# Startup transposes in shared PSUM banks, a new base time for the planner, and two output tiles kept in PSUM: one change to a planned two-branch attention kernel

## The chip, the cores and the metric

The kernel runs on one core of a Trainium2 chip. The core has five engines that run side by side, each with its own instruction queue, worked off in order: TensorE (matrix products and transposes, written to PSUM), VectorE (DVE), ScalarE (ACT), GpSimd (POOL) and SyncE (SP, which here only issues DMAs). They wait for each other by semaphores. PSUM has eight banks of 128 partitions by 512 fp32 values; a matrix product can land only there, and only VectorE and ScalarE take results out of it here. The metric is the time of one execution in microseconds, as the device measures it; lower is better.

## The reference

Two attention branches run on the same input `x` of 2048 tokens by 512 values (bf16), 32 heads of 16, and are mixed by a gate per token:

```python
x = A_x
g = _sigmoid((x * gate_w).sum(-1, keepdims=True))
a = _A_ref(x, A_wqkv, A_wo)
b = _B_ref(x, B_wqkv, B_wo)
return g * a + (1 - g) * b
```

Branch A is full attention, without a mask:

```python
qkv = (x @ wqkv).reshape(B, S, 3, H, Dh).transpose(2, 0, 3, 1, 4)
scores = jnp.einsum("bhqd,bhkd->bhqk", q, k) * (Dh ** -0.5)
p = _softmax(scores, axis=-1)
o = jnp.einsum("bhqk,bhkd->bhqd", p, v)
return o.transpose(0, 2, 1, 3).reshape(B, S, D) @ wo
```

Branch B is local: each token sees itself and seven earlier tokens in steps of two (`W, dil = 8, 2`), with its own weights.

## The kernel before, in words

**Branch A.** Heads are taken four at a time (a group; `NG = 8`), queries 512 at a time (a chunk; `NC = 4`), which gives 32 periods. In a period the scores of a head against 128 keys (a unit) are one matmul of 32 rows, and 64 units make the period. Units are put together in sets of three and two (`set_sizes=(3, 2)`). A wide set lands in PSUM ring `rA` (three banks), a narrow one in `rB` (two banks); ScalarE takes the exponential of a whole set in one instruction into `pT`; then TensorE multiplies four units at a time with the values and adds into an accumulator of one bank. There are 684 sets. In most periods some units do not go through ScalarE: VectorE makes an approximate exponential of them by integer arithmetic (`p1`, and three shifted copies `sh`), and TensorE adds all four versions up.

The softmax is not shifted by its own maximum. The kernel instead appends to each key a bound on the keys' size: `k_bound` reduces the largest key values (`mx`), moves them between partitions with two tiny matmuls with a permutation (`sw`), takes the negative maximum (`ng`), and fills it into the key rows (`fill`). No score matmul of a head group can start before its fill.

**Branch B.** Tiles of 128 tokens. TensorE projects, VectorE copies keys and values to `kvs`, SyncE stores them to DRAM (`kv_scr`) and gathers them back shifted (`ksh`, `vsh`), GpSimd multiplies and adds, ScalarE does a small exponential per tile, some sums run as accumulating DMAs. TensorE transposes the result into `obt`.

**The start.** SyncE issues the loads: first chunk of `x`, A's key weights, the other three chunks, A's query and value weights, the gate vector and B's weights. TensorE transposes each chunk into `xT` in two halves (L612 to L637): the first half goes to ring `rA` and is copied out by ScalarE, the second half to ring `rB` and is copied out by VectorE. Then come the four key projections of head group 0, the first query projection (`q_proj(0, ...)`), the first value blocks (`v_proj(0, 4, ...)`), the bound and its fill, and the first score set.

**The end.** The last four output tiles cannot be finished before the last head groups are. For each of them the part that is already known is summed in PSUM in the last two periods and copied by VectorE into unused room of the key buffer as fp32 (`fa`). After the last exponential VectorE transposes the accumulator (`po1`), takes reciprocals, scales by the gate and transposes back (`po3`); TensorE does one more matmul per tile (`tail`), VectorE adds the kept part (`t_ev`), and SyncE stores the tile.

**What sets the order.** The order on each engine is not the order of the source. Every step is an `op` with an engine, an assumed duration, a due time, an earliest time (`rel`), dependences and the buffers that it takes (`tok`). `list_schedule` plays this through with its own clock: whenever an engine could start something, it picks the startable step with the earliest due time. For loads the assumed time until the data lies in place is `lat`. Due times of branch A follow from a base time `T0` and a pace of 0.465 per unit (`S0` are the starts of the periods); those of branch B follow from `b_start` and do not depend on `T0`. `misc` and `acc` name three shared PSUM banks; accumulators, projections and the scores for VectorE take them in turn. Where TensorE would be thin, the planner puts in matmuls with zeros (`zeros`). The order that comes out is then fixed by a chain of dependences on each engine. So a changed due time or duration at one place can move steps everywhere.

Of the kernel before, what the change touches and what calls it, by code (L numbers as in the profile page):

```python
# [9 lines left out]
ALU = mybir.AluOpType  # L10
AX = mybir.AxisListType
# [17 lines left out]
NG = 8  # L29
# [272 lines left out]
def kernel(  # L302
# [49 lines left out]
    def chain(bi):  # L352
        return chain_on("pe", bi)
# [21 lines left out]
    def mm_ct(out, lhsT, rhs, start, stop):  # L375
        mm(out, lhsT, rhs, start, stop)
# [32 lines left out]
    T0 = 17.0  # L409
# [76 lines left out]
    kmax = const.tile([128, NG], FP32, name="kmax")  # L486
# [89 lines left out]
    o_x[0] = op("sp", 0.5, load_x(0), -9.0, alloc=[xtok[0]], lat=5.5)  # L576
    o_wk = op("sp", 0.5, load_w(1), -8.9, lat=6.5)
    o_x[1] = op("sp", 0.5, load_x(1), -8.8, alloc=[xtok[1]], lat=7.5)
    o_x[2] = op("sp", 0.5, load_x(2), -8.7, alloc=[xtok[2]], lat=9.5)
    o_x[3] = op("sp", 0.5, load_x(3), -8.6, alloc=[xtok[3]], lat=11.0)  # L580
    o_wq = op("sp", 0.5, load_w(0), -8.5, lat=12.5)
    o_wv = op("sp", 0.5, load_w(2), -8.4, lat=13.0)
    o_bw = op("sp", 1.0, load_bw, -8.3, lat=19.0)
# [28 lines left out]
    o_xt = []  # L612
    for sc in range(NC):
        st = {}
        tk2 = [tok("rA", 1), tok("rB", 1)]

        def tr(half, sc=sc, st=st):
            def s():
                st[half] = ps.tile([128, 2, QW], BF16, tag=("rA", "rB")[half], bufs=1, name="pxt")
                for c in range(2):  # L620
                    for tt in range(TPC):
                        chain(nc.tensor.transpose(out=st[half][:, c, tt * 128:(tt + 1) * 128],  # L622
                                                  in_=xld[sc][:, tt, (2 * half + c) * 128:(2 * half + c + 1) * 128],
                                                  identity=ident[:]))
            return s

        def ev(half, sc=sc, st=st):
            def s():
                dst = xT[:, 2 * half:2 * half + 2, sc * QW:(sc + 1) * QW]
                src = st[half][:]  # L630
                if half == 0:
                    A.copy(out=dst, in_=src)
                else:
                    V.tensor_copy(out=dst, in_=src)
            return s
        t1 = op("pe", 0.6, tr(0), -5.0 + sc, deps=[o_x[sc], o_id], alloc=[tk2[0]], use=[xtok[sc]])
        t2 = op("pe", 0.6, tr(1), -4.9 + sc, deps=[t1], alloc=[tk2[1]], use=[xtok[sc]])  # L637
        o_xt.append([op("act", 1.0, ev(0), -5.0 + sc, deps=[t1], use=[tk2[0]]),
                     op("dve", 0.61, ev(1), -4.9 + sc, deps=[t2], use=[tk2[1]])])
# [24 lines left out]
    def k_bound(i, dl):  # L664
# [3 lines left out]
        def mx():  # L668
            V.tensor_reduce(out=kmax[:, i:i + 1], in_=kmax_all[:, i, :], axis=AX.X, op=ALU.max)
            V.tensor_copy(out=kmax_b[:, i:i + 1], in_=kmax[:, i:i + 1])  # L670
# [15 lines left out]
        a = op("dve", 0.4, mx, dl - 2.5, deps=o_kc[i])  # L686
# [61 lines left out]
    v_proj(0, 4, 0, 8, "misc", 6.0)  # L748
    v_proj(0, 4, 8, 8, "misc", 7.0)
# [9 lines left out]
    def q_proj(pi, tag, dl, rel=0.0):  # L759
# [15 lines left out]
        def ev():  # L775
            V.tensor_copy(out=qt_tiles[pi][:], in_=st["p1"][:])
# [7 lines left out]
        c = op("dve", 0.61, ev, dl - 0.5, deps=[b], use=[tk, tq])  # L784
        o_q[pi] = op("dve", 0.0, ab, dl, deps=[c], use=[tq], parts=SB(QW))

    q_proj(0, "acc", 2.5)
# [46 lines left out]
    for pi in range(2, NP, 2):  # L834
        q_pair(pi, S0[pi] - QD, S0[pi - 2] - 2.0)
# [558 lines left out]
    for t in range(NT):  # L1394
# [6 lines left out]
        dl = E + (4.0 + 4.0 * tt if last else 2.0 + 4.0 * tt)  # L1401

        def ab_part(k0, st=st, c_=c_, tt=tt, nh=nh):
            def s():
                if k0 == 0:
                    st["pf"] = misc_ps([128, D])
                for k in range(k0, min(k0 + 2, DC + nh)):
                    if k < DC:
                        mm_ct(st["pf"], obt_tiles[c_][:, k, tt * 128:(tt + 1) * 128], bwo[:, k, :], k == 0, k == DC + nh - 1)
                    else:  # L1410
                        mm_ct(st["pf"], oat_tiles[c_][:, k - DC, tt * 128:(tt + 1) * 128], woarr[:, k - DC, :], False,
                              k == DC + nh - 1)
            return s
# [13 lines left out]
        for k0 in range(0, DC + nh, 2):  # L1427
            nk = min(2, DC + nh - k0)
            a = op("pe", WAVE(nk), ab_part(k0), dl - 2.0 + 0.3 * k0, full=nk,
                   deps=[a] if k0 else [o_oat[NG * c_ + ng - 1], o_wo] + o_obt[t:t + 1],  # L1430
                   alloc=[tk] if k0 == 0 else [], use=([tk] if k0 else []) + [oat_tok[c_], obt_tok[c_]])
        if not last:
            tos = tok("osb", 2)
            a = op("dve", 0.61, ab_ev, dl, deps=[a], alloc=[tos], use=[tk])
            op("sp", 0.6, dout, dl + 1, deps=[a], use=[tos], lat=2.2)
        else:
            a = op("dve", 0.61, ab_ev, dl, deps=[a], use=[tk])
            tag = ("misc", "acc", "rB", "rA")[tt]
            otag = ("osb", "osb", "kvs", "kvs")[tt]
            tk, tos = tok(tag, 2 if tag == "misc" else 1), tok(otag, 2)  # L1440
            E2 = S0[NP]
# [9 lines left out]
            b = op("dve", 0.61, t_ev, E2 + 1 + tt, deps=[b, a], alloc=[tos], use=[tk])  # L1451
            op("sp", 0.6, dout, E2 + 2 + tt, deps=[b], use=[tos], lat=2.2)

# [45 lines left out]
```

## Time and profile before

| | us |
|---|---|
| median of three runs | 819.31 |
| the three runs | 816.12, 819.31, 819.32 |
| the profiled execution, its own time | 815.66 |
| its span | 813.9 |
| first exponential of branch A starts | 19.58 |
| last exponential of branch A starts, ends | 804.48, 805.13 |
| ScalarE busy | 785.7 (97%) |
| TensorE busy | 751.9 (92%) |
| VectorE busy | 690.2 (85%) |
| GpSimd busy | 633.8 (78%) |

Times in the profile count from the start of the span. A group line gives the source line of the helper that recorded the instruction, engine, operation, result and operands, shapes and how often; then busy time and mean duration, and after the second bar the idle time of the engine just before and what ended it. All VectorE, ScalarE and GpSimd operations go through one helper (L364) and all matmuls through another (L373), so the names of the tiles tell them apart: `ring` are score sets, `pT` exponentials, `misc_ps` whatever lies in the shared banks, `pxt` transposed chunks of `x`, `xld` and `pd_a` the loaded chunks (the fourth lies in `pd_a`), `wk` the copy of key weights, `z` zeros. In timelines the first two numbers of a line are start and duration of a run of equal instructions, the bracket at its end idle time before the run.

### The profile page before, as it was taken

The numbers are of one execution on the slowest core, as the hardware profiler recorded it, in microseconds if no ns is written. First come the engines' busy times: TensorE is split into PE (matmuls) and PEld (weight loads), VectorE is DVE, ScalarE is ACT, GpSimd is POOL, SyncE is SP. The second block draws the span as 40 slices with busy tenths as digits, with TensorE's granted clock in tenths as the row PEclk, the third lists the DMA queues.
The fourth block names the chain that finished last, engine by engine and source line by source line (L and its number), as shares of the span: only waits on it lengthen the run. The fifth ranks groups of instructions, "written<-read, shape, count | busy, mean of one in ns | idle before, by whom it ended". The sixth has DMA issues, their size and how long they took to land.

```text
span 813.9 us, 18012 instructions
## 1 busy us (share of the span) xinstructions
PE 751.9 (92%) x6962; PEld 246.2 (30%) x7018; DVE 690.2 (85%) x1080; ACT 785.7 (97%) x706; POOL 633.8 (78%) x1058
## 2 busy tenths in 40 slices
PE   8999999999999998999889999989989999898996
PEld 4333334324222222222222222323222222222322
DVE  5646776897887999989989899997988899898887
ACT  2999999999999999999999999999999999999995
POOL 3098969799899999999997794989769419899910
PEclk9999999999999999999999999999999999999998
DMA  7503071533544344443524407162440521522000
GB/s 261 143 2 118 2 172 50 135 86 100 132 118 112 95 114 131 103 127 93 149 55 119 126 17 171 45 162 54 91 125 12 124 92 49 147 59 72 1 2 27
DMA packets 58886, 77.22 MB, mean 95 GB/s; under 512 B 3744, under 2 KB 50848, under 8 KB 58800
## 3 DMA queue, kind: packets, MB, share of 16 engines
q1 hardware_dynamic: 52752, 54.05, 21.5%
q0 software_dynamic: 6048, 22.02, 14.6%
q8 instruction: 55, 0.90, 0.5%
q14 instruction: 31, 0.25, 0.1%
HBM read 43.78 MB, written 10.26 MB: 66 GB/s over the span
## 4 chain that ended last, share of the span: by engine, by line
ACT 46%; PE 28%; issue 18%; POOL 4%; DVE 3%; DMA 1%; SPq 0%; DVEq 0%; ACTq 0%
ACT pT L364 46%; PE misc_ps L373 19%; PE ring L373 8%; POOL prod L364 2%; POOL av L364 1%; DMA xld<-in_A_x_dram 1%; DVE kt_all L364 1%; ACT lg L364 1%; DVE pd_a L364 1%; PE pxt L622 0%; DVE wkv L364 0%; DVE osb L364 0%; POOL lg L364 0%; POOL obb L364 0%; DVE accT L364 0%
## 5 line engine op out<-in xcount | busy, mean ns | idle before, releaser
L364 ACT ACTIVATE pT<-ring 128x1536 bf16<-128x1536 f32 (+1 forms) x684 | 778.6, 1319 | 10.3 <-PE ring L373 9.8
L373 PE MATMUL ring<-qt,kt_all 32*128 32x512 bf16 x1709 | 270.4, 382 | 46.1 <-ACT pT L364 36.7
L364 POOL TENSOR_TENSOR prod<-ksh,qb 128x256 f32<-128x256 bf16 x256 | 175.8, 745 | 65.2 <-DMA ksh<-kv_scr 32.8
L373 PE MATMUL misc_ps<-pT,vp_all 128*17 128x512 bf16 (+1 forms) x1709 | 208.6, 383 | 0.1
L373 PEld LDWEIGHTS <-kt_all 32*128 32x128 bf16 x2048 | 88.4, 91 | 299.7 <-issue 290.4
L364 DVE TENSOR_SCALAR pd_a<-wkv 128x1536 uint16<-128x1536 uint16 x192 | 175.3, 941 | 1.7 <-PE misc_ps L373 0.6
L364 POOL TENSOR_TENSOR prod<-prod 128x256 f32<-128x256 f32 (+1 forms) x256 | 167.1, 668 | 5.8
L364 DVE TENSOR_SCALAR wkv<-misc_ps 128x512 uint16<-128x512 f32 x192 | 129.2, 683 | 27.9 <-PE misc_ps L373 23.1
L373 PE MATMUL misc_ps<-z 128*32 128x512 bf16 x421 | 138.9, 386 | 1.6 <-DVE z L364 1.6
L364 DVE TENSOR_SCALAR pd_a<-dt_a 128x1536 uint16<-128x1536 uint16 x147 | 135.3, 944 | 1.0
L373 PE MATMUL misc_ps<-pd_a,vd_all 128*17 128x512 bf16 x1017 | 131.3, 381 | 0.2
L373 PE MATMUL misc_ps<-qt,kt_all 32*128 32x512 bf16 x339 | 125.2, 380 | 2.4 <-DVE wkv L364 0.7
L364 DVE TENSOR_SCALAR dt_a<-misc_ps 128x512 uint16<-128x512 f32 x147 | 99.1, 685 | 18.3 <-PE misc_ps L373 16.9
L364 POOL TENSOR_TENSOR prod<-vsh,lg 128x256 f32<-128x256 bf16 x128 | 81.7, 739 | 0.0
L364 POOL TENSOR_TENSOR av<-vsh,lg 128x256 f32<-128x256 bf16 x128 | 79.6, 657 | 0.0
L373 PEld LDWEIGHTS <-vp_all 128*17 128x17 bf16 (+1 forms) x2048 | 54.7, 88 | 80.1 <-issue 66.2
L373 PE MATMUL misc_ps<-bw,xT 128*128 128x512 bf16 x164 | 50.8, 384 | 2.6 <-issue 1.1
L373 PEld LDWEIGHTS <-z 128*32 128x32 bf16 x421 | 37.0, 96 | 50.7 <-issue 28.1
L373 PEld LDWEIGHTS <-vd_all 128*17 128x17 bf16 x1017 | 35.1, 88 | 47.6 <-issue 38.0
L373 PEld LDWEIGHTS <-xT 128*128 128x128 bf16 x576 | 30.2, 99 | 33.4 <-issue 29.2
L364 POOL DMA_DIRECT2D av<-av x14 | 12.3, 882 | 33.3 <-DMA av<-prod 33.3
L373 PE MATMUL misc_ps<-xT,wkv 128*32 128x512 bf16 x384 | 37.9, 382 | 0.0
(89 smaller groups left out, 584.2 us busy)
## 6 DMA issues: line engine op xcount, KB each, us to landing
ksh<-kv_scr SPq DMA_DIRECT2D x32, 512.0 KB
vsh<-kv_scr SPq DMA_DIRECT2D x32, 512.0 KB
av<-prod POOLq DMA_DIRECT2D x28, 512.0 KB, 5.8
av<-av POOLq DMA_DIRECT2D x14, 512.0 KB, 5.0
kv_scr<-kvs SPq DMA_DIRECT2D x16, 256.0 KB
qt<-q_scr SPq DMA_DIRECT2D x30, 128.0 KB
out_dram<-osb SPq DMA_DIRECT2D x16, 128.0 KB
q_scr<-qs SPq DMA_DIRECT2D x15, 128.0 KB
```

The source lines that it names most:

```text
L364: return chain_on(key, f(*a, **k))
L373: return chain(nc.tensor.matmul(out, lhsT=lhsT, rhs=rhs, start=start, stop=stop, **kw))
```

## The change

1. `T0` is 14 in place of 17, and the assumed landing times of the first eight loads are shorter (4.8 to 16.0 in place of 5.5 to 19.0).
2. Of the four chunks of `x`, the first and third are transposed into the rings as before, the second and fourth into the shared banks. Their due times are 20 earlier for the transposes and far earlier for the copies, and each half must come after the one before it.
3. `mx` reduces straight into bf16; the fp32 copy and the conversion go, for all eight head groups.
4. The first value blocks get an earliest time of 16.5. The first query projection is due 2.5 earlier and is copied by ScalarE instead of VectorE. The query pairs get an earliest time of at least 18.
5. Of the last four output tiles, the first two (`pin`) are no longer copied to `fa`: they stay in a shared bank with an open sum. The first is due at the end of the last period, behind the last scores for VectorE and all but the last eight value products; the second stands behind all of them. Their last matmul adds into the same bank, ScalarE copies the bank to the output tile, and the store is issued by SyncE for the first and by ScalarE for the second. The other two tiles do as before, in the rings.

```diff
-    T0 = 17.0
+    T0 = 14.0
...
-    o_x[0] = op("sp", 0.5, load_x(0), -9.0, alloc=[xtok[0]], lat=5.5)
...
-    o_bw = op("sp", 1.0, load_bw, -8.3, lat=19.0)
+    o_x[0] = op("sp", 0.5, load_x(0), -9.0, alloc=[xtok[0]], lat=4.8)
...
+    o_bw = op("sp", 1.0, load_bw, -8.3, lat=16.0)
...
+    last_tr = [None]
     for sc in range(NC):
+        ev_ops = []
+        for half in range(2):
+            st = {}
+            tk = tok("misc", 2) if sc % 2 else tok(("rA", "rB")[half], 1)
+
+            def tr(sc=sc, half=half, st=st):
+                st["x"] = misc_ps([128, 2, QW], BF16) if sc % 2 else ps.tile([128, 2, QW], BF16, tag=("rA", "rB")[half], bufs=1, name="pxt")
...
+            def ev(sc=sc, half=half, st=st):
+                (V.tensor_copy if half else A.copy)(out=xT[:, 2 * half:2 * half + 2, sc * QW:(sc + 1) * QW], in_=st["x"][:])
+            t_ = op("pe", 0.6, tr, -25.0 + sc + 0.1 * half, deps=[o_x[sc], o_id], after=[last_tr[0]], alloc=[tk], use=[xtok[sc]])
+            last_tr[0] = t_
+            ev_ops.append(op("dve" if half else "act", 0.61 if half else 1.0, ev, -100.0 + sc, deps=[t_], use=[tk]))
+        o_xt.append(ev_ops)
...
         def mx():
-            V.tensor_reduce(out=kmax[:, i:i + 1], in_=kmax_all[:, i, :], axis=AX.X, op=ALU.max)
-            V.tensor_copy(out=kmax_b[:, i:i + 1], in_=kmax[:, i:i + 1])
+            V.tensor_reduce(out=kmax_b[:, i:i + 1], in_=kmax_all[:, i, :], axis=AX.X, op=ALU.max)
...
-    v_proj(0, 4, 0, 8, "misc", 6.0)
-    v_proj(0, 4, 8, 8, "misc", 7.0)
+    v_proj(0, 4, 0, 8, "misc", 6.0, rel=16.5)
+    v_proj(0, 4, 8, 8, "misc", 7.0, rel=16.5)
...
-            V.tensor_copy(out=qt_tiles[pi][:], in_=st["p1"][:])
+            (V.tensor_copy if pi else A.copy)(out=qt_tiles[pi][:], in_=st["p1"][:])
...
-        c = op("dve", 0.61, ev, dl - 0.5, deps=[b], use=[tk, tq])
+        c = op("dve" if pi else "act", 0.61, ev, dl - 0.5, deps=[b], use=[tk, tq])
...
-    q_proj(0, "acc", 2.5)
+    q_proj(0, "acc", 0.0)
...
-        q_pair(pi, S0[pi] - QD, S0[pi - 2] - 2.0)
+        q_pair(pi, S0[pi] - QD, max(18.0, S0[pi - 2] - 2.0))
...
+        pin = last and tt < 2
+        if pin:
+            dl = S0[NP] - 1.0
...
-                              k == DC + nh - 1)
+                              k == DC + nh - 1 and not pin)
...
+                   deps=[a] if k0 else [o_oat[NG * c_ + ng - 1], o_wo] + ([d_last[0]] + o_pv[NP - 1][:len(o_pv[NP - 1]) - (8, 0)[tt]] if pin else []) + o_obt[t:t + 1],
...
+        elif pin:
+            tos = tok("osb", 2)
+
+            def tail(st=st, c_=c_, tt=tt):
+                mm_ct(st["pf"], oat_tiles[c_][:, NH - 1, tt * 128:(tt + 1) * 128], woarr[:, NH - 1, :], False, True)
+
+            def t_ev(st=st):
+                st["o"] = work.tile([128, D], BF16, name="osb", tag="osb", bufs=2)
+                A.copy(out=st["o"][:, 0:D], in_=st["pf"][:])
+            b = op("pe", 0.26, tail, S0[NP] + 60 + tt, deps=[o_oat[NP - 1], a], use=[tk, oat_tok[c_]])
+            b = op("act", 0.6, t_ev, S0[NP] + 3 + tt, deps=[b, a], alloc=[tos], use=[tk])
+
+            def dout_a(st=st, t=t):
+                A.dma_start(out=out2d[t * 128:(t + 1) * 128, :], in_=st["o"][:, 0:D])
+            op(("sp", "act")[tt], 0.6, (dout, dout_a)[tt], S0[NP] + 4 + tt, deps=[b], use=[tos], lat=2.2)
         else:
             a = op("dve", 0.61, ab_ev, dl, deps=[a], use=[tk])
-            tag = ("misc", "acc", "rB", "rA")[tt]
-            otag = ("osb", "osb", "kvs", "kvs")[tt]
+            tag = ("rB", "rA")[tt - 2]
+            otag = "kvs"
             tk, tos = tok(tag, 2 if tag == "misc" else 1), tok(otag, 2)
-            E2 = S0[NP]
+            E2 = S0[NP] - 2.0
```

## The prediction

> **What bounds the kernel now.** I read the page first, then ScalarE's timeline, then VectorE's between 14 and 19 us, then the end, then the granted clock by stretch.
>
> ```profile
> span 813.9 us, 18012 instructions
> PE 751.9 (92%) x6962; PEld 246.2 (30%) x7018; DVE 690.2 (85%) x1080; ACT 785.7 (97%) x706; POOL 633.8 (78%) x1058
> ...
> ACT 46%; PE 28%; issue 18%; POOL 4%; DVE 3%; DMA 1%; SPq 0%; DVEq 0%; ACTq 0%
> ...
> L364 ACT ACTIVATE pT<-ring 128x1536 bf16<-128x1536 f32 (+1 forms) x684 | 778.6, 1319 | 10.3 <-PE ring L373 9.8
> ```
>
> ScalarE is busy 97% of the span with 684 exponentials, and half of its idle time is one wait of 5.1 us before the first. So the span is a head (until the first exponential), a stream, and an end.
>
> ```profile
> 13.48 1.01 ACT L364 COPY xT<-pxt 128x1024 bf16<-128x1024 bf16 x1 [0.69 <-PE pxt L622]
> 19.58 21.92 ACT L364 ACTIVATE pT<-ring 128x1536 bf16<-128x1536 f32 x19 [5.09 <-PE ring L373]
> ```
>
> The head is 19.58 us. The last exponential begins at 804.48 and ends at 805.13. By their starts in the trace, undisturbed exponentials follow each other every 1.331 us (three units) and 0.904 us (two units); over that floor the stream loses 16.2 us (0.31 us taken off at each of the 17 places where another ScalarE operation stands between). Almost all of it is a wide set whose scores came late after a narrow one. That is all a better order can win in the stream.
>
> ```profile
> 15.78 0.75 DVE L364 TENSOR_SCALAR_CACHE_REDUCE kt_all<-misc_ps,rowc 128x512 bf16<-128x512 f32 x1
> ...
> 16.57 0.16 DVE L364 TENSOR_REDUCE kmax<-kmax_all 128x1 f32<-128x4 f32 x1
> 16.77 0.16 DVE L364 CAST kmax_b<-kmax 128x1 bf16<-128x1 f32 x1
> 16.84 0.68 DVE L364 CAST qt<-misc_ps 128x512 bf16<-128x512 f32 x1
> 17.55 0.35 DVE L364 TENSOR_SCALAR qt<-qt,qmask 128x256 uint32<-128x256 uint32 x1
> 17.82 0.69 DVE L364 CAST vp_all<-misc_ps 128x512 bf16<-128x512 f32 x1
> 18.42 0.21 DVE L364 SCALAR_TENSOR_TENSOR negk<-misc_ps,rowc 128x1 f32<-128x1 f32 x1
> 18.67 0.41 DVE L364 TENSOR_SCALAR kt_all<-kt_all,rowc,negk 128x512 bf16<-128x512 bf16 x1
> ```
>
> The head's last part is one queue, VectorE's: last key copy, maximum, query copy, mask, value copy, bound, fill.
>
> ```profile
> 805.81 0.72 DVE L364 STREAM_TRANSPOSE accT<-misc_ps 128x512 f32<-128x512 f32 x1 [0.86 <-PE misc_ps L373]
> ...
> 808.29 1.38 PE L373 MATMUL misc_ps<-woarr,oat 128*128 128x512 bf16 x3 [2.05 <-DVE oat L364]
> 808.72 2.48 DVE L364 TENSOR_TENSOR osb<-misc_ps,kt_all 128x512 bf16<-128x512 f32 x4 [0.48 <-PE misc_ps L373]
> 809.44 2.12 SPq L364 DMA_DIRECT2D out_dram<-osb  x4
> ```
>
> The end is 8.76 us: five VectorE steps, four matmuls, four VectorE adds one after another, their stores (the last issued at 811.23) and 2.66 us until all is over.
>
> ```profile
> 136.42:139.83 3.41, 2.43 (x17) 0.58 (x16) 3.33 (x8) 2.83 (x3) 3.33 (x7) 1.00 0.00 0
> 139.83:143.25 3.42, 3.06 (x22) 1.81 (x23) 2.62 (x5) 2.82 (x3) 3.11 (x7) 0.50 0.02 5
> ```
>
> The columns are busy times of PE, PEld, DVE, ACT and POOL, then the granted clock. A thin stretch is followed by a 3.41 us stretch at half clock; the two late starts in it (140.58, 143.6) cost 0.73 + 0.61 us.
>
> **The change, part by part.** The program built from the changed kernel gives the order on each engine; durations are those of before.
>
> *Transposes.* Loads are issued in the same order, and by their landings (8.23, 9.72, 11.24, 12.73 us for x's second to fourth chunk and the query weights) set the pace. TensorE now runs: chunk 1's transposes 8.27 to 9.27; the first key projection to 10.13 (16 matmuls, four passes of 0.215); half the second to 10.56; chunk 2's transposes to 11.56 (16 take 1.0); chunk 3's, no longer behind the ScalarE copy that ended at 12.78, to 12.56 instead of 13.89; the other half to 12.99. The third key projection waits for the bank that ScalarE's copy of chunk 3 leaves (12.24 + 1.01), so 13.30 to 14.16. Now the first query projection stands before the fourth key projection: 14.16 to 15.02, then 15.02 to 15.88. Its VectorE copy follows the start by 1.09, as at 14.69 and 15.78: 16.11, against 15.78 before, 0.33 later.
>
> *Bound and query copy.* One reduction in place of two saves 0.20 (16.57 to 16.77). The query copy goes to ScalarE (0.7 off VectorE, 16.84 to 17.55), hidden on a ScalarE idle from 14.5; without that cover it would cost its 0.7. From the key copy: maximum +0.79 = 16.90; mask at 17.0; value copy at 17.27; bound at 17.87; fill at 18.12; scores and first exponential 0.91 later, 19.03. The later bounds lose one small VectorE operation each, 1.1 us in all, beside the stream: nothing.
>
> *Values wait for the bound.* In the order they do not: the first value block still stands before the two bound matmuls, and its copy before the bound on VectorE. Worth 0. **Head: -0.55** (from +0.3, the late key copy kept and nothing else won, to -1.1, were the value copy not in the way).
>
> *Gate matmuls* (64 of one column) move from sets 16 to 24 up to sets 2 to 8, where value and B projections stood. ScalarE never waited there (0.3 us over the floor before 40 us), so nothing is won, but TensorE gets thin: between 20 and 24 us some three full passes, and the stretch that lost the clock had 3.75 (score matmuls count a quarter each). I count one half-clock stretch more or less: +0.8 (0 to +2.6, two of the 1.3 measured).
>
> *The stream.* The earlier base time (14 for 17) re-deals everything. Counting passes between two score sets: after a narrow set, groups of over 5.5 passes fall from 41 to 31; with the excess that each size showed before (0.04 us at 4 to 5 passes, 0.09 at 5 to 6, 0.12 at 6 to 6.5, 0.4 above 7, 1.1 above 8) the stream gains 0.85 (from -5 to +4: that 16.2 came to lie at either side).
>
> *B's path.* The first B keys and values are copied about seven sets later, so SyncE's first store, both gathers behind it and GpSimd's first product (39.80) come about 5.6 us later. GpSimd has the cover: it waited 33.3 us for its own accumulating transfers and 32.8 for gathers. If that cover is gone, see the second rival.
>
> *The end.* The last TensorE matmul waits for the last exponential alone, so VectorE starts 0.46 after it rather than 0.68. Tile 0 is accumulated inside the stream; tile 1's seven matmuls (1.5 us) run beside VectorE's 2.5 us, as do three fillers; at half clock they would run 1.6 us over. The final matmuls start 2.94 after the last exponential; tiles 2 and 3 are added on VectorE (3.37 and 3.97), tiles 0 and 1 copied on ScalarE (3.80 and 4.45; 0.65 each, the 128x512 exponential, between nothing shorter and the 1.01 of twice the width). SyncE issues at 4.1, 4.5 and 4.85; ScalarE's own queue issues the last at 5.15, where before it was 6.10. Nothing is queued behind the new waits on ScalarE. **End: -0.95** (0 if a store from ScalarE costs a microsecond more, to -1.2).
>
> Sum: -0.55 + 0.8 - 0.85 - 0.95 = -1.55, so 814.1 against the profiled execution's 815.66. That execution is the quickest of the four known (815.66, 816.12, 819.31, 819.32; mean 817.6), and I cannot say what parts them; the median of after may fall in either pair, so I forecast 817.6 - 1.55 = **816.0**.
>
> **Rivals.** *Cold head.* The three filler matmuls between the transposes of chunks 0 and 1 (6.93) are gone. If transposes do not keep the clock up, 6.71 to 10.12 holds four passes, near the 3.75 that lost it. Then K projections take 1.72 and transposes 1.67 until 16.95; the third key projection ends at 16.91, the query's at 17.8, the fourth at 18.67, and the first exponential falls at 21.8: +2.8 on the forecast, 818.8. Against it: the clock rose at 6.71 after a stretch with two fillers and fourteen transposes, and not at 3.30 after one with more fillers. The Trainium skill (TensorE: Matmul & The Clock Gate, Part 4: PE-mode transpose) says that transposes do not count as work for the clock; by that rule this rival would hold, and the rise at 6.71 speaks against it.
>
> *GpSimd late, and slower than before.* ScalarE and TensorE wait in order for it. Before, the softmax input was ready 0.9 to 8.7 us ahead, and the transposes of B's output 0.5 to 15. By the new order (set numbers and GpSimd's work before each) the eleventh tile would have about -0.5 us left, less what remains of the 5.6. It pays 0.5 to 6.1 (-0.5 less the whole 5.6); I take 5.0, most of the delay still there: 821.0. From 3.3 us on it is slower than 819.31. For it: 0.9 left already before. Against: just before that tile GpSimd idled 4.6 and 6.4 us on transfers.
>
> *The stream is dealt better* than passes tell: a third of its 16.2 us gone, -5: 811.0 to 811.9. For it: the heaviest groups (8.2 and 8.5 passes, 1.19 and 1.11 us lost) are partly moved into the first sets.
>
> **How the numbers follow.** Forecast 0.43, better stream 0.25, GpSimd late 0.18, cold head 0.14. About 0.5% (4.1 us) is what a measurement of this kernel can tell from no change; against 819.31 the bounds are 815.2 and 823.4. The better stream is faster (0.25), as is the forecast where the median falls in the lower pair (0.12 of 0.43). Beyond 823.4 lie GpSimd late and cold head where the median falls in the upper pair (1.7 us above the mean) and a little more is lost (0.14). The rest is 0.49. The range, 811 to 822, reaches from the better stream to GpSimd's top.
>
> **What would show it.** The first exponential at 19.0 (21.8: cold head); the granted clock at one from 6.7 us to the gate matmuls, half once after them; no ScalarE wait on its softmax input; last store 5.2 us after the last exponential. I am wrong if the first exponential moves by over a microsecond, if the stream between first and last exponential differs from 784.9 by over 3, or if the ScalarE copies end the program later than VectorE's four adds did.

## The result and the profile after

The changed kernel took 820.16 us (median of 22 runs, 817.79 to 823.33), the kernel before 817.72 us in the same comparison (22 runs, 815.73 to 820.82). The ratio is 1.0037 with a 95% interval of 1.0024 to 1.0049: slower, by about 3 us (the two medians lie 2.4 us apart), where 816.0 us and no slowing were forecast. The profiled execution took 819.93 us, its span 818.2 us, against 815.66 and 813.9 before. The profiled execution of before was quicker than all 22 timed ones of that kernel, so the differences between the two profiles add up to 4.3 us, more than the medians show.

The page of the kernel after, its engine totals, its chain of waits and its group of exponentials:

```profile
span 818.2 us, 17960 instructions
...
PE 755.3 (92%) x6935; PEld 246.3 (30%) x6994; DVE 683.8 (84%) x1067; ACT 787.7 (96%) x709; POOL 632.2 (77%) x1058
...
ACT 48%; PE 25%; issue 21%; DVE 4%; POOL 1%; DMA 1%; SPq 0%; ACTq 0%
...
L364 ACT ACTIVATE pT<-ring 128x1536 bf16<-128x1536 f32 (+1 forms) x684 | 779.1, 1327 | 10.9 <-PE ring L373 9.1
```

VectorE did less (683.8 us against 690.2) and ScalarE's exponentials hardly changed (779.1 against 778.6). ScalarE still sets the length, so the question is again head, stream and end. Measured by the exponentials' starts:

| profiled execution | before | after | difference |
|---|---|---|---|
| first exponential begins | 19.58 | 21.67 | +2.09 |
| first to last exponential | 784.90 | 787.70 | +2.80 |
| last exponential's own time | 0.65 | 0.74 | +0.09 |
| its end to the end of the span | 8.76 | 8.04 | -0.72 |

*The head.* ScalarE's timeline, then VectorE's, of the kernel after:

```profile
13.70 1.01 ACT L364 COPY xT<-pxt 128x1024 bf16<-128x1024 bf16 x1 [3.49 <-PE pxt L623]
...
21.67 3.71 ACT L364 ACTIVATE pT<-ring 128x1536 bf16<-128x1536 f32 x3 [3.17 <-PE ring L373]
```

```profile
18.78 0.75 DVE L364 TENSOR_SCALAR_CACHE_REDUCE kt_all<-misc_ps,rowc 128x512 bf16<-128x512 f32 x1 [0.97 <-PE misc_ps L373]
...
19.58 0.16 DVE L364 TENSOR_REDUCE kmax_b<-kmax_all 128x1 bf16<-128x4 f32 x1
19.65 0.35 DVE L364 TENSOR_SCALAR qt<-qt,qmask 128x256 uint32<-128x256 uint32 x1
19.91 0.69 DVE L364 CAST vp_all<-misc_ps 128x512 bf16<-128x512 f32 x1
20.51 0.22 DVE L364 SCALAR_TENSOR_TENSOR negk<-misc_ps,rowc 128x1 f32<-128x1 f32 x1
```

From the last key copy on everything went as worked out: copy at 18.78, exponential 2.89 later (19.03 - 16.11 = 2.92 was forecast). What is late is the key copy itself, by 2.67 us, and TensorE's timeline tells why:

```profile
5.11 1.89 PE L623 MATMUL pxt<-ident,xld 128*128 128x128 bf16 x16 [0.35 <-DMA xld<-in_A_x_dram]
8.12 1.89 PE L623 MATMUL misc_ps<-ident,xld 128*128 128x128 bf16 x16 [1.12 <-DMA xld<-in_A_x_dram]
9.94 0.62 PE L373 MATMUL misc_ps<-xT,wkv 128*32 128x512 bf16 x3
...
10.34 0.64 PE L373 MATMUL misc_ps<-xT,wkv 128*32 128x512 bf16 x3
...
10.77 0.64 PE L373 MATMUL misc_ps<-xT,wkv 128*32 128x512 bf16 x3
```

Sixteen transposes take 1.89 us (1.07 at 8.27 before), and one pass of a projection follows the next after 0.40 to 0.43 us (0.215 before): half speed. The clock's first record at full speed stands at 14.16 us; before, it stood at 6.71. This is the rival called cold head, which put the first exponential at 21.8.

*The end.* The kernel after, by its timeline:

```profile
810.58 0.72 DVE L364 STREAM_TRANSPOSE accT<-misc_ps 128x512 f32<-128x512 f32 x1 [3.56 <-PE misc_ps L373]
...
813.06 1.04 PE L373 MATMUL misc_ps<-woarr,oat 128*128 128x512 bf16 x4
813.48 1.29 DVE L364 TENSOR_TENSOR osb<-misc_ps,kt_all 128x512 bf16<-128x512 f32 x2 [0.48 <-PE misc_ps L373]
813.91 1.07 ACT L364 CAST osb<-misc_ps 128x512 bf16<-128x512 f32 x2 [3.80 <-PE misc_ps L373]
814.20 1.32 SPq L364 DMA_DIRECT2D out_dram<-osb  x3
815.02 0.41 ACTq L364 DMA_DIRECT2D out_dram<-osb  x1
```

Two adds run on VectorE, two copies beside them on ScalarE, and the last store is issued 4.91 us after the last exponential's end (5.15 was forecast, 6.10 stood before).

*The stream.* An exponential is called late here by the time that its start lies behind the floor of the prediction (1.331 us after a wide set, 0.904 after a narrow one, 0.31 more where another ScalarE operation stands between). Of the late starts four groups stand out, by the number of the exponential: 145 to 152 (2.1 us together), 270 (1.6), 382 to 386 (1.6), and 24 to 30 (1.2). The half-clock stretches are at 195.07 and 468.14 us, 3.41 us each. The forecast drop behind the gate matmuls is not in this execution. Exponential 270 is late by 1.6 us with the clock at full, ScalarE idle for 1.30 of them, and that is new; ScalarE, VectorE, GpSimd and TensorE around it:

```profile
337.19 2.36 ACT L364 ACTIVATE pT<-ring 128x1536 bf16<-128x1536 f32 x2 [1.30 <-PE ring L373]
```

```profile
331.40 0.69 DVE L364 CAST qs<-misc_ps 128x512 bf16<-128x512 f32 x1
332.12 2.22 DVE L364 TENSOR_SCALAR qa<-qs 128x256 uint32<-128x256 uint32 x1
334.26 0.94 DVE L364 TENSOR_SCALAR pd_a<-wkv 128x1536 uint16<-128x1536 uint16 x1
335.12 0.68 DVE L364 TENSOR_SCALAR wkv<-misc_ps 128x512 uint16<-128x512 f32 x1
```

```profile
329.99 2.84 POOL L364 TENSOR_TENSOR prod<-ksh,qb 128x256 f32<-128x256 bf16 x4
332.51 2.47 POOL L364 TENSOR_TENSOR prod<-prod 128x256 f32<-128x256 f32 x3
```

```profile
335.85 0.37 PE L373 MATMUL misc_ps<-qt,kt_all 32*128 32x512 bf16 x1 [1.27 <-DVE wkv L364]
```

The sign mask of a query pair, SBUF to SBUF, takes 2.22 us beside a row of seven GpSimd operations; where GpSimd ran no tensor operation beside it, it took 0.28 to 0.29 us (all 32 such masks in the twelve profiles that have it). VectorE's next steps are late by that, TensorE waits 1.27 us for one of them, and ScalarE waits for the scores queued behind it. That made a second theory beside the clock.

### The profile page after: what moved, and what is told of

It reads as the page before. It is cut to its first block, busy times and chain, and to the rows that moved or that the text cites. A ratio compares the mean times of both kernels' runs of the same rounds, so it can differ in the third digit from the quotient of the medians.

```text
span 818.2 us, 17960 instructions
## 1 busy us (share of the span) xinstructions
PE 755.3 (92%) x6935; PEld 246.3 (30%) x6994; DVE 683.8 (84%) x1067; ACT 787.7 (96%) x709; POOL 632.2 (77%) x1058
## 4 chain that ended last, share of the span: by engine, by line
ACT 48%; PE 25%; issue 21%; DVE 4%; POOL 1%; DMA 1%; SPq 0%; ACTq 0%
ACT pT L364 47%; PE misc_ps L373 17%; PE ring L373 8%; DVE pd_a L364 1%; DMA xld<-in_A_x_dram 1%; DVE wkv L364 1%; ACT lg L364 1%; POOL prod L364 1%; POOL av L364 0%; DVE dt_a L364 0%; PE misc_ps L623 0%; DVE qa L364 0%; PE pxt L623 0%; DVE accT L364 0%; DVE kt_all L364 0%
## 5 line engine op out<-in xcount | busy, mean ns | idle before, releaser
L364 ACT ACTIVATE pT<-ring 128x1536 bf16<-128x1536 f32 (+1 forms) x684 | 779.1, 1327 | 10.9 <-PE ring L373 9.1
L373 PE MATMUL misc_ps<-pT,vp_all 128*17 128x512 bf16 (+1 forms) x1709 | 204.7, 385 | 1.3 <-DVE wkv L364 0.5
L373 PE MATMUL misc_ps<-z 128*32 128x512 bf16 x397 | 131.8, 389 | 1.6 <-DVE z L364 1.6
L364 POOL TENSOR_TENSOR prod<-vsh,lg 128x256 f32<-128x256 bf16 x128 | 84.4, 763 | 0.0
L364 POOL TENSOR_TENSOR av<-vsh,lg 128x256 f32<-128x256 bf16 x128 | 77.6, 642 | 0.0
L373 PEld LDWEIGHTS <-z 128*32 128x32 bf16 x397 | 35.2, 96 | 47.7 <-issue 26.4
L364 DVE TENSOR_SCALAR_CACHE_REDUCE kt_all<-misc_ps,rowc 128x512 bf16<-128x512 f32 x32 | 23.9, 746 | 27.3 <-PE misc_ps L373 27.3
L373 PE MATMUL misc_ps<-xT,wkv 128*32 128x512 bf16 x384 | 39.6, 393 | 0.4 <-DVE kt_all L364 0.2
```

The costliest lines, as they stand in the source:

```text
L364: return chain_on(key, f(*a, **k))
L373: return chain(nc.tensor.matmul(out, lhsT=lhsT, rhs=rhs, start=start, stop=stop, **kw))
```

## The experiments

Every kernel below was timed against runs of the kernel before on the same chip. In the table, head is the start of the first exponential and stream the time from the first to the last, both of one profiled execution (the kernel before: 19.58 and 784.90); "clock lost" names the exponentials near which a half-clock stretch begins in it. Half is the mean over the runs of the time at half clock, 2 x (1 - granted clock) x 815 us; the kernel before has 7.1, 8.1, 9.4 and 7.8 us in the four comparisons, of which its profile shows 5.0 at the very end of the program, where little hangs on it (1.9 for after). What lies ahead of the first record is not in it.

| run | ratio to before (95%) | head | stream | clock lost at | half, us |
|---|---|---|---|---|---|
| after, first profile | 1.0037 (1.0024 to 1.0049) | 21.67 | 787.70 | 146, 382 | 16.0 |
| e5 after again | 1.0048 (1.0025 to 1.0071) | 18.82 | 791.95 | 1, 146, 382 | 17.5 |
| e1 after, head fillers | 1.0035 (1.0017 to 1.0053) | 18.78 | 789.78 | 2, 269 | 14.9 |
| e6 and gate fillers | 1.0038 (1.0023 to 1.0052) | 19.00 | 789.31 | 146, 382, 642 | 13.6 |
| e7 and 15 masks | 1.0005 (0.9993 to 1.0017) | 18.66 | 787.27 | 145 | 4.6 |
| e9 and thin places filled | 1.0025 (1.0006 to 1.0044) | 18.67 | 791.09 | 246, 353 | 4.6 |
| e8 after, 15 masks only | 1.0014 (0.9996 to 1.0032) | 18.82 | 790.95 | 1, 146, 382 | 7.6 |
| e13 after, 2 masks only | 1.0007 (0.9990 to 1.0024) | 21.70 | 785.15 | 146 | 9.2 |
| e12 head and gate fillers, 2 masks | 0.9981 (0.9963 to 0.9998) | 19.01 | 785.36 | 145 | 5.3 |
| e14 the same, fewer gate fillers | 0.9997 (0.9982 to 1.0011) | 18.69 | 786.87 | 1, 146 | 8.8 |
| e2 before, no head fillers | 1.0030 (1.0014 to 1.0045) | 19.56 | 786.09 | 100 | 12.0 |
| e15 the same, second profile | one run | 21.02 | 785.60 | head, 100 | |
| e3 before, end only | 0.9999 (0.9987 to 1.0012) | 19.28 | 784.62 | none | 3.1 |
| e4 before, base time 14 only | 1.0003 (0.9987 to 1.0018) | 19.52 | 787.66 | 16, 331, 435 | 10.3 |
| e11 before, 15 masks only | 1.0033 (1.0017 to 1.0049) | 19.49 | 789.11 | 100 | 6.5 |
| e10 before, end, 15 masks, thin filled | 1.0028 (1.0014 to 1.0041) | 19.54 | 788.35 | none | 2.6 |

### The head: fillers put back, fillers taken away

```diff
                 if sc == 1 and half == 0:
+                    tz = misc_ps([128, QW])
+                    for _ in range(3):
+                        mm(tz[0:32, :], z32[:], z_bc, True, True, tile_position=(0, 0))
```

> The changed kernel with three filler matmuls (128x512, the size of the others) put back in front of the transposes of chunk 1; nothing else moves. Cold-head theory: TensorE's wait of 1.1 us for the second chunk is what kept the clock at half until 14.16 us. With the fillers the clock rises by 7 to 8 us, the first exponential begins at 19.0 to 19.6 instead of 21.73, and the whole is 2.1 to 2.7 us quicker than the changed kernel: ratio to the kernel before about 1.001. Rival, the new order of the transposes and of the first projections is itself what is slow: the first exponential stays at 21.5 or later, ratio 1.004. The 2.8 us that the stream lost should stay by either.

(The 21.73 in these texts is the 21.67 of the table, counted from another zero.) The head did what the cold-head theory says: the clock rose at 6.75 us, the first exponential began at 18.78. The whole did not: 1.0035. The stream grew by another 2.1 us, in two places. The granted clock by stretch (busy times of PE, PEld, DVE, ACT, POOL, then the clock) in the run with fillers, first at the gate matmuls, then at the mask:

```profile
20.40:23.81 3.41, 2.49 (x47) 1.27 (x43) 1.85 (x4) 3.41 (x4) 0.00 (x0) 1.00 0.15 42
23.81:27.23 3.42, 3.36 (x22) 0.94 (x20) 0.00 (x0) 1.85 (x2) 0.00 (x0) 0.50 0.32 96
```

```profile
331.01:334.43 3.42, 1.96 (x15) 0.44 (x17) 3.39 (x7) 2.26 (x3) 1.63 (x3) 1.00 0.26 72
334.43:337.84 3.41, 3.41 (x22) 0.47 (x20) 2.96 (x5) 2.48 (x2) 3.32 (x6) 0.50 0.56 153
337.84:341.25 3.41, 3.41 (x25) 0.67 (x23) 2.79 (x5) 3.15 (x3) 3.33 (x6) 0.50 0.98 221
341.25:344.67 3.42, 3.42 (x25) 0.72 (x24) 2.36 (x4) 2.20 (x3) 1.50 (x3) 0.50 0.09 16
```

The forecast drop behind the gate matmuls comes when the clock is up before them, and makes exponential 6 late by 2.42 us. And TensorE's wait for VectorE's queue, held up by the mask, thins its work so far (1.96 us busy of 3.42) that the clock goes for three stretches: 2.8 us more behind the 1.6.

> The kernel before without its three filler matmuls in front of the transposes of chunk 1; nothing else moves. Cold-head theory: the clock no longer rises at 6.7 us, the key projections take 0.43 us a pass and the first exponential begins 1.5 to 2.5 us later than 19.58, ratio about 1.0025. Rival, transposes alone keep the clock up: the first exponential stays within 0.3 us of 19.58, ratio 1.000.

```diff
+    cut = [o for o in order if o.name == "zeros" and 5.0 < o.t < 9.0]
     for o in order:
+        if o in cut:
+            continue
```

1.0030, close to the price that the theory gave, but the profile showed an ordinary head and a longer half-clock stretch at set 100. So the same program was profiled once more:

> A second look at the kernel before without the three fillers of its head; its median was 1.7 us longer, but its one profile had a clock that rose at 5.92 us and a first exponential at 19.56. Cold-head theory: the missing fillers make the head cold in part of the executions, so this one has either the same head or a half-clock stretch between 6 and 14 us with the first exponential at 21 to 22 us. If the head never turns cold, the 1.7 us lie elsewhere.

```profile
4.70:8.11 3.41, 1.12 (x17) 0.90 (x16) 1.23 (x3) 1.01 (x1) 2.15 (x4) 1.00 1.09 352
8.11:11.53 3.42, 3.40 (x32) 2.24 (x36) 0.69 (x1) 1.01 (x1) 0.00 (x0) 0.50 1.10 349
```

Here the clock had risen at 4.70 and was lost again at 8.11, behind a stretch that held chunk 0's transposes, a wait of 1.95 us for chunk 1 and nothing else; the first exponential began at 21.02. The same program gave 19.56 in the other profile. The clock changes in steps of 3.41 us whose place relative to the program differs from execution to execution; the missing fillers make a cold head possible, and the place of the steps decides. In the six profiles without fillers a step falls at 5.34, 5.92 and 6.27 us where the head stayed warm (e5, e2, e8), and at 3.92, 3.96 and 4.70 where it was cold (the first profile of after, e13, e15); with fillers, steps at 4.55 and 4.87 (e12, e6) went with a warm head. All eleven profiles of kernels with the fillers (the one before among them) have a warm head, 18.66 to 19.58; of the six without, three do. The Trainium skill (TensorE: Matmul & The Clock Gate, Part 1: The HAM clock gate) says that the window behind these steps runs free of the program's start; the profiles agree, with first records at full speed anywhere from 4.55 to 6.87 us in kernels that begin alike.

### The changed kernel profiled again

> The changed kernel itself, a second profiled execution and times beside the next two. If the cold head hangs on the order of the transposes alone, the clock again rises only after 10 us and the first exponential begins at 21 to 22 us; if it hangs on where the clock's own 3.4 us windows happen to lie, it may begin anywhere from 18.8 to 21.8. The wait of 1.6 us near 334 us should be there again (it stands in the first profile and in that with fillers); ratio to before 1.003 to 1.004.

The clock rose at 5.34 and the first exponential began at 18.82, 2.85 us earlier than in the first profile of the same program. It bought nothing: behind the gate matmuls the clock was lost for two stretches (exponential 6 late by 2.99), and the mask at 155 us took 4.83 us, the longest of all:

```profile
154.67 4.83 DVE L364 TENSOR_SCALAR qa<-qs 128x256 uint32<-128x256 uint32 x1
```

```profile
155.17 2.83 POOL L364 TENSOR_TENSOR prod<-ksh,qb 128x256 f32<-128x256 bf16 x4
157.69 1.65 POOL L364 TENSOR_TENSOR prod<-prod 128x256 f32<-128x256 f32 x2
```

```profile
161.29 1.45 ACT L364 ACTIVATE pT<-ring 128x1536 bf16<-128x1536 f32 x1 [2.07 <-PE ring L373]
```

It ended at 159.50, just after GpSimd's row did (159.34), and ScalarE was late by 2.38 us at exponential 118. The wait at 270 came back, 1.59 us. The mask had begun 0.50 us ahead of the row, while GpSimd issued a DMA; what held it then is not known.

### The end alone, the base time alone

> The kernel before with the change's last part alone (two of the last four output tiles kept in banks, copied by ScalarE, one stored from ScalarE's queue); the order of all earlier work is the same. The theory is that this part won what the two profiles show, 0.75 us from the last exponential to the end: 8.0 us instead of 8.76, head and stream unchanged, ratio 0.999. Rival, that the 0.75 was the difference between two single executions: 8.5 to 9.0 us, ratio 1.000.

The edit is the diff's last three hunks on the kernel before; the order of all earlier work stays. The end took 8.05 us, head and stream 19.28 and 784.62: the gain is there, 0.71 us. The ratio, 0.9999 with an interval 0.0025 wide, cannot show so little.

> The kernel before with the earlier base time alone (14 for 17, with the bound of 18 on the release of the query pairs): head and end as before, the gate matmuls in sets 2 to 8, everything in the stream dealt anew. Theory, the new deal is what the stream lost by: first exponential at 19.6, stream from first to last exponential 786.5 to 789 us instead of 784.9, ratio 1.003. Rival, the stream lost its 2.8 us through the clock (two half-clock stretches met by chance): stream 784 to 786 us, ratio 1.000.

```diff
-    T0 = 17.0
+    T0 = 14.0
...
-        q_pair(pi, S0[pi] - QD, S0[pi - 2] - 2.0)
+        q_pair(pi, S0[pi] - QD, max(18.0, S0[pi - 2] - 2.0))
```

The profile bears out the theory (787.66 us, gate matmuls early, clock lost at 16, 331 and 435, a mask of 3.11 us at 208.8 with ScalarE 1.83 us late), the median does not: 1.0003. Single executions of this kernel lie between 813.5 and 820.4 us, and one profile of a stream is one draw. So the base time alone is not shown to lose; it is a deal in which masks and thin places fall elsewhere.

### Gate fillers and masks

> The changed kernel with the three fillers of the head and, in front of each of the four blocks of 16 gate matmuls, two more fillers of 480 columns. Theory: in the run with fillers the early clock was lost again at 23.8 us, in the thin stretch that the gate matmuls make, and cost 2.4 us there; filled up, that drop does not occur, stream 2 to 2.4 us shorter than the 789.8 with head fillers alone, ratio 1.001 to 1.002. Rival, the thin stretch is not what drops the clock: the half-clock window is again between 20 and 30 us, ratio 1.0035.

```diff
-                st_g["zp"] = misc_ps([128, NT])
+                st_g["zp"] = misc_ps([128, QW])
+            for _ in range(2):
+                mm(st_g["zp"][0:32, 32:QW], z32[:], z_bc480, True, True, tile_position=(0, 0))
```

(z_bc480 stands here for a column of zeros read 480 times.) The drop at 20 to 30 us did not occur, but exponentials 4 and 6 are late by 0.49 and 0.42 us for the fillers, the head by 0.2, and the profile has three drops elsewhere. The ratio did not move: 1.0038. The gate block was a cost in executions with a warm head, not the main one.

> The same, and the sign mask of the query pairs (128x256 uint32, SBUF to SBUF, 0.28 to 3.1 us long) replaced by a VectorE operation that reads the pair from PSUM (larger of the negated PSUM value and the bf16 copy), right behind the pair's copy. Theory: the mask at 332 us took 2.22 us because it ran beside a row of GpSimd tensor operations, and it is what made ScalarE wait 1.6 us near 334 and then cost the clock (10.2 us at half, 3 us more, in the run with fillers). From PSUM it takes 0.7 us whenever it runs: no ScalarE wait over 0.6 us near 334, no half-clock stretch there, stream 783 to 785.5 us, ratio 0.997 to 0.999. Rival, the wait near 334 comes from the dealt order and not from the length of the mask: it stays at over 1 us and the ratio is that of the run with gate fillers.

```diff
+            st["a"] = work.tile([128, QW], BF16, name="qa", tag="qa", bufs=1)
+            V.scalar_tensor_tensor(out=st["a"][:], in0=st["p"][:], scalar=-1.0, in1=st["s"][:], op0=ALU.mult, op1=ALU.max)
...
-            st["a"] = work.tile([128, QW], BF16, name="qa", tag="qa", bufs=1)
-            V.tensor_scalar(out=st["a"][:].bitcast(U32), in0=st["s"][:].bitcast(U32), scalar1=0x7FFF7FFF, scalar2=None,
-                            op0=ALU.bitwise_and)
+            pass
```

Every mask now takes 0.69 us, exponential 270 is on time, and against the run before it on the same chip the median falls from 819.59 to 817.01 us; the mean time at half clock falls from 13.6 to 4.6 us. The stream, 787.27, and the ratio, 1.0005, stayed above the 783 to 785.5 and the 0.997 to 0.999 that were expected.

> The changed kernel with the mask of the query pairs from PSUM alone, no fillers. If the mask beside GpSimd's row is the largest part of what the change lost, this alone takes off about 2.6 us of the 3 to 4 (the step from the run with gate fillers to the run with gate fillers and mask), ratio to before 1.001 to 1.002; the head stays that of the changed kernel: 18.8 us with a clock drop behind it near 22 us, or 21.7 without. Rival, the step was the fillers' and the mask's together: ratio 1.003 or more.

The same masks without any filler: 1.0014, as expected, and with 118 and 270 on time. The clock was lost at the gate again (2.34 us).

> The kernel before with the mask from PSUM alone. In its profile only one of 15 masks was over 0.8 us (1.18 at 210.6 us), and the longer operation adds 0.2 to 0.4 us to the others, off ScalarE's path. By the theory that the collision belongs to the changed order, nothing is won here: ratio 0.9995 to 1.0005. Rival, the masks cost as much in either order: ratio 0.997.

This one fell outside both expectations: 1.0033, slower. The masks together took 10.4 us on VectorE instead of 7.7, and the stream grew by 4.2 us in many small pieces. So the 15 long masks have a price of their own, and if they cost as much in the changed order, what they won there was larger than the 2.6 us. Why 2.7 us on VectorE cost 4.2 us on ScalarE was not settled.

> The changed kernel with those two masks from PSUM and nothing else. Theory, these two collisions with the clock they cost are the largest part of what the stream lost: 1.6 us at set 270 and up to 2.4 us at set 118 gone, 3 to 4 us quicker than the changed kernel, ratio 0.999 to 1.000. Rival, they are only the 1.6 us seen in every profile: ratio 1.002. If they are no cause: 1.004.

```diff
+            if pi in (6, 14):
+                st["a"] = work.tile([128, QW], BF16, name="qa", tag="qa", bufs=1)
+                V.scalar_tensor_tensor(out=st["a"][:], in0=st["p"][:], scalar=-1.0, in1=st["s"][:], op0=ALU.mult, op1=ALU.max)
...
+            if pi in (6, 14):
+                return
```

Only the two pairs whose masks ran beside GpSimd's rows; the order of every engine stays. The row of seven is still there, the mask is not held:

```profile
332.21 0.69 DVE L364 SCALAR_TENSOR_TENSOR qa<-misc_ps,qs 128x512 bf16<-128x512 f32 x1
332.82 0.94 DVE L364 TENSOR_SCALAR pd_a<-wkv 128x1536 uint16<-128x1536 uint16 x1
```

```profile
330.09 2.84 POOL L364 TENSOR_TENSOR prod<-ksh,qb 128x256 f32<-128x256 bf16 x4
332.62 2.46 POOL L364 TENSOR_TENSOR prod<-prod 128x256 f32<-128x256 f32 x3
```

```profile
332.50 7.09 ACT L364 ACTIVATE pT<-ring 128x1024 bf16<-128x1024 f32 x6
```

The ratio is 1.0007 instead of 1.0037 or 1.0048. It lies between what the theory and its rival said, and its interval, 0.9990 to 1.0024, holds both. This execution had the same cold head (21.70) and the same drop at 146 as the first profile of after, so the streams can be set side by side: 785.15 against 787.70, 2.55 us. Of these 1.5 us are the mask at 270. The other 1.0 us lie at 382 to 386, where the clock was not lost this time, and that is not shown to be the masks' doing: the clock's steps fall alike in both executions, and the program was 1.5 us ahead by then.

> The changed kernel with head fillers, gate fillers, and the mask from PSUM for only the two query pairs whose masks ran beside GpSimd's rows (third and seventh, at 155 and 332 us); the other 13 as they were. All 15 from PSUM made the changed kernel with fillers 2.6 us quicker but the unchanged kernel 2.7 us slower, so two alone should keep the gain without that cost: 2 to 4 us quicker than with all 15, ratio to before 0.996 to 0.998. Rival, the gain came from elsewhere among the 15: ratio 1.0025 or more, with ScalarE late by over 1 us at set 270.

0.9981 (0.9963 to 0.9998), 815.15 us against 816.15: head 19.01, stream 785.36, end 8.05. It is the quickest run of all, and its interval ends just below the kernel before. This kernel is that of e6 with the two masks changed and nothing else, and e6 stood at 1.0038 (1.0023 to 1.0052): the intervals are far apart. So the two masks are shown to be the cause of most of the slowing, though the two runs were on different chips, each beside the kernel before. The time at half clock fell with them, from 13.6 to 5.3 us. The new operation differs from the mask in its operands' place, in kind and in number type; which of these frees it was not tested.

> As the run before the last, with three gate fillers (two in front of the first block, one in front of the second) instead of eight. The eight made ScalarE late by 0.49 and 0.42 us at sets 4 and 6 in each profile; three should cost 0.3 us at most and still keep the clock: 0.3 to 0.8 us quicker, ratio 0.995 to 0.9975. If three don't keep it, a half-clock stretch stands between 20 and 28 us again and it is 1 to 2 us slower than with eight.

Three gate fillers don't hold the clock: lost at 23.30 us, exponential 6 late by 2.30 us, 0.9997. With the eight, exponentials 4 and 6 are late by 0.9 us together, and e12 is still 1.1 us quicker.

### Thin places filled

> The run with fillers, gate fillers and mask, plus two filler matmuls in front of each value product of sets 142 to 148 and 379 to 385 (18 in all), the two places at which the changed order's profiles lost the clock most often (sets 145 to 149 in four of five, 382 to 385 in three of five). Theory: these are thin stretches, and filled up they keep the clock; no half-clock stretch near 190 and 464 us, 1 to 1.5 us quicker than the run before it, ratio 0.998 to 0.9995. Rival, the clock is lost there because ScalarE is late (0.66 us at set 145, 0.61 at 382), not because TensorE is thin: the drops stay, ratio 1.0005 or above.

```diff
+        if o.fill and o.of is not None and any(a <= o.of <= b for a, b in ((142, 148), (379, 385))):
+            o.filled += 2
```

The clock held at both places, as the theory says, and nothing was won: 145 and 382 were late all the same (0.67 and 0.83), the clock went at 246 and 353 instead, and the ratio was 1.0025, above the 1.0005 of the run without them (on another chip). So those late starts are not the clock's doing, and the clock that is kept in one place can go in another. Neither expectation held whole.

> The kernel before in its own order, with the change's end, the mask from PSUM, and two fillers in front of each value product of sets 97 to 102, where two of three profiles of that order lost the clock (sets 100 to 103). Expected: head 19.3 to 19.6, no half-clock stretch near 137 us, end 8.05 us; ratio 0.997 to 0.9985, the quickest so far. If the clock is not held by those six fillers: 0.999.

The six fillers held the clock (none lost), but the 15 masks cost what they cost in e11: 1.0028. The expectation was written before that price was known.

## Why the prediction was wrong

**B's path: the step that failed.** The prediction saw that GpSimd's work would come later against the rest (its first product began at 48.25 us in the first profile, 8.5 later than before, where 5.6 was forecast) and asked only who waits for GpSimd's results. Those had cover, as it said: no ScalarE wait on a softmax input in any profile, and the rival called GpSimd late did not come. What runs beside GpSimd's work it put at nothing, without a reason. Two masks on VectorE, 0.3 us long when alone, met rows of GpSimd operations and took 1.9 to 4.8 us. Undoing those two alone took away the 1.6 us at exponential 270, and by the ratios 0.3% (e13 against after) to 0.57% (e12 against e6) of the time. That they met because B's work and the query pairs moved by different amounts is read from the two orders (the seventh mask began at 352.4 us before and at 332.1 after, the GpSimd row that it met stands at 330.0); no run moved one of them alone.

A rule that the prediction should have weighed stands in the Trainium skill (SBUF — State Buffer, SBUF: two separate sides): VectorE and GpSimd share one pair of SBUF ports, locked for a whole instruction, and a VectorE instruction that needs that pair beside VectorE's own waits for it. The traces agree in that the mask waited when it read SBUF alone and not when it read PSUM. They show more than the rule gives, as far as GpSimd's rough spans tell. No operation of those rows takes over 1.0 us, but each begins 0.3 us before the one ahead has ended, and the mask ended 0.16 us after the last of them: at 334.34 behind 334.18 in the first profile, at 159.50 behind 159.34 in e5. Where GpSimd's operations overlapped by less than 0.15 us, the row did not hold the mask: 79 masks had over 1 us of such work still ahead and took 0.28 to 0.89 us.

**Head, -0.55.** The terms were right and their condition was not. With a warm head the first exponential began at 18.8 us (e5, e8) where 19.03 was forecast; with a cold one at 21.67 to 21.70, where the rival said 21.8. The sentence that failed is "the rise at 6.71 speaks against it": one execution's rise was read as what the program does, but the place of the clock's steps varies, and the fillers were what made the rise safe. Whether transposes count for the clock, as the Trainium skill denies (TensorE: Matmul & The Clock Gate, Part 4: PE-mode transpose), no run here settles: the stretch that lost the clock, 4.70 to 8.11 us, held 16 transposes but also a wait of 1.95 us.

**Gate matmuls, +0.8.** The mechanism was right, the size off: exponential 6 was late by 2.3 to 3.0 us in each of the four profiles with a warm head and no or few gate fillers (e1, e5, e8, e14). Behind a cold head no half-clock stretch came there, and exponential 6 was late by 0.86 (after, e13), so the drop itself cost 1.4 to 2.1. A warm head was thus worth little in the changed kernel, because it led into this drop. The two late starts from which the prediction took its 1.3 us begin at 142.2 and 145.1; its 140.58 and 143.6 are the starts ahead of them.

**The stream, -0.85.** It lost 2.80 us. Of these the mask at 270 explains 1.5, and the half-clock stretch at 468 us, which e13 did not have, 1.0. What remains, +0.25 to +0.5 (e13, e12), is near nothing, and counting passes between score sets forecast none of it. The rival of a better deal did not come.

**Bound, query copy, values.** From the last key copy to the first exponential 2.89 us against 2.92: right.

**The end, -0.95.** Right in kind, -0.72, and shown alone (-0.71). The last store was issued sooner than forecast (4.9 us after the last exponential's end against 5.15 after, counted the same way), but from a store on ScalarE's queue to the end of the span it took 3.1 us where 2.66 had stood: about half of the microsecond that the prediction allowed for that store.

**The execution used.** The sum went from the quickest profiled execution and was moved to a mean, 817.6, near the 817.72 that 22 runs gave. The range, 811 to 822, held 820.16 by luck: its upper part was there for GpSimd being late, which did not come. The sign was wrong. Of the three signs of being wrong that the prediction named, one came: the first exponential moved by 2.09 us, while the stream's 2.80 stayed just inside its 3.

## What to carry to other kernels

When work on GpSimd moves, ask which operations of VectorE between SBUF tiles it will now run beside, not only who waits for its results: a 0.3 us mask can last as long as the whole row. Read from the trace which operations do so, since not all of them wait. Fillers that bridge a wait for a load protect against a clock whose steps fall differently in each execution, so one profile with a warm clock does not show that they can go. Where single executions spread by 5 us, compare profiles event by event, at the same exponential, and let the medians decide.

## What the runs showed of the hardware

- A VectorE mask of 128x256 uint32 in SBUF takes 0.28 to 0.29 us with no GpSimd tensor operation beside it (32 of 174 masks), 0.28 to 0.70 beside one, up to 1.94 beside three, 2.20 to 2.23 beside five (four cases), 3.11 and 4.83 beside six (a mask that lasts longer also meets more of them). Of 16 masks that began with 0.9 us or more still to come of a GpSimd row whose operations overlap by 0.3 us, 12 ended 0.16 to 0.17 us after the row, one just before its end, and three, all at one query pair in the order of before, were not held (0.28). The operation that reads PSUM and SBUF in place of the mask took 0.69 us beside the same row.
- Not every VectorE operation between SBUF tiles is held. The 5763 of 128x1536 uint16 (`pd_a`) in the 17 profiles took 0.89 to 0.96 us, whatever GpSimd ran; the fill of the bound (`kt_all`, 128x2048 bf16) took 0.80 to 0.81 with no GpSimd tensor operation beside it and 2.89 to 3.11 beside four.
- The granted clock falls for whole stretches of 3.41 us. In the 35 runs of the kernel before that stood beside e1 to e4 each further microsecond at half clock goes with 0.39 us of time (a line fitted to their clocks and times); in the runs of that kernel beside the other three groups it is 0.35, 0.43 and 0.44.
- Full speed was lost without any long pause of TensorE: behind stretches of 3.41 us in which it was busy 1.96, 2.49, 2.62 and even 3.03 and 3.19 us (e14), with no pause over 1.3 us. In the last three of these many matmuls were short, or used a quarter of the rows. And a half-clock stretch in which TensorE was busy throughout ended the state at 24 and 195 us, while at 334 us it took three. What decides was not found.
